# Block-sparse attention on attended blocks alone in F32 tiles, with an f16 first product in the feed-forward part

## The chip, the cores and the metric

One core of one Trainium2 chip. The metric is the device time of one launch in microseconds (us). The kernel before took 909.31 us (median of 3 runs, 909.0 to 910.31).

## The reference

`q`, `k`, `v` are 4 batches x 8 heads x 768 tokens x 64, in float32; `sampled_blocks` gives 3 random key blocks for each of 24 query blocks of 32 tokens.

```python
scores = scale * np.matmul(q, k.transpose(0, 1, 3, 2))
mask = np.abs(blk_i - blk_j) <= 1
mask = mask | (blk_i == 0) | (blk_j == 0) | (blk_i == n_blocks - 1) | (blk_j == n_blocks - 1)
for qb in range(n_blocks):
    for kb in sampled_blocks[qb]:
        mask[qb * 32:(qb + 1) * 32, kb * 32:(kb + 1) * 32] = True
scores = np.where(mask, scores, -1e9); scores -= scores.max(-1)
attn = np.exp(scores); attn /= attn.sum(-1) + 1e-9
x = (attn @ v) as 3072 tokens x 512
h = x @ w_in                      # 512 x 2048
out = (h - np.tanh(h)) @ w_out    # 2048 x 512
```

So the first and last query block see all 24 key blocks, and each of the other 22 sees at most 8: itself and its two neighbours, the two end blocks, three random ones.

## The kernel before, in words

There are two stretches in one program. In the first, attention runs head by head, and a part of the feed-forward work is woven in; in the second, only feed-forward work is left.

Attention before computes all 768 x 768 scores of a head, with the mask as extra rows of the product. Values are split in a high and a low half, so that two or three products at the faster matmul rates stand for one float32 product. For each head `smax` (L479) makes scores with the queries on the partitions, `maxima` (L485) takes their row maxima, `scores` (L520, L521) makes them again with the keys on the partitions and the maximum taken off in an extra row. Then ScalarE exponentiates 128 x 768 at a time (`expo`, L527) and makes an f16 high half (`p_high`, L531), GpSimd makes the low half (`p_low`, L540), and `accum` (L563, L566, L567) multiplies by V in f16, 36 products of 65 columns for a step. One step is 256 keys of one head; there are 96 steps. `norm` (L574 to L578) divides by the sums and `spill` sends the result to DRAM (`xscr`), from where the feed-forward part loads it.

The feed-forward part cuts the tokens in 6 chunks `n` of 512 and the 2048 hidden columns in 16 tiles `ft`. One unit is (n, ft). Its first product is 12 matmuls of 512 columns (`h_part`, L915, three split products for each of four rows of `w_in`, in fp32r), its gate is 5 instructions on VectorE, 5 on ScalarE and one on GpSimd (`g_part`), its second product is 12 matmuls (`o_mm`, L950 to L952). All of `w_in` and `w_out` come as 64-bit words; VectorE turns each tile to float32 in three instructions (`convert_part`), and the tile is then split. Before, 4 tiles are made in the first stretch (`NRES`), two more are stored, and 10 are made in the second (`RATE` gives how many per unit). 16 of the 96 first products are in the first stretch, and 14 of the second ones. Segments (`SEGS`) give the order of the 82 units of the second stretch.

The order on each engine is written out (`ORDER`, one string an engine), and the engines wait for each other by semaphores. Nothing of the second stretch is put ahead of anything of the first on any engine. DMAs are issued by SyncE, one after the other, in that order too. `KeepBusy` puts idle matmuls on ones (L245) where the planner expects TensorE to be idle.

Of the kernel before, what the change touches and what calls it, by code (L numbers as in the profile page):

```python
# [22 lines left out]
P = 128  # L23
B, H, S, D = 4, 8, 768, 64
NB, BLK = 24, 32
T = S // P
# [6 lines left out]
SEGS = ((3, 2, 6), (4, 0, 6), (5, 0, 16), (4, 6, 16), (3, 6, 16), (2, 4, 16), (1, 4, 16), (0, 4, 16))  # L33
RATE = 1.0
# [6 lines left out]
        "#$%#%#%#%######)()##+&##$$&#%##'&####)($$#%##*%)##(##))&#++#'&(#'##''##&)(##+*'#,##*'&###*')##(##%##%##$#+%###"  # L41
        "$#%*##(%#*#&###(###'#&#%##*%##$#+####'####((#################$$$%##$$$###$######$$$%%''&''&(#&%%#%%%%%#%%&&%#$"
        '%#$,$$$####&#$#&####2$$$$###$$#$#$$+#%%$#$$#%$$#$$###%%#######%%####%###################$$%%$#&$#%%$$$&#$$#$$%'
        "%$##########$###$$%%%%%%&&&#&&'&&##%%&&%#$#%##%##(%$###############$#$$#(##$$#*&$$%%$#$$$#$$###%#$##########*%"
        "%$$$##$$##$$#%%##$$##$$#%&&$#'###%%##$%%#*#&&$#$#$$#'########%#$###%#$#(%##&###$&$$#$#$###$#%##&%'##'##%%###%#"
        "#&#####$###$$$%##%%##%%$%%#######/#$$##)%#+&#(%#$&##%#%#%#(#&#($'##'$'$#&&###''$%+%$($&####$%%#$(#$%###('&$#$#"
        "$&%#$$'#&$####$%#&###$#%$#'&%(##&#%###%)&#%$#&#$%)'$%('#')$#&'#$#&%&###%#%##%$%&&'$%&'#%###$#%#&##%#&%##$$##%&"
        "$'#'$##&%##&&*$&#(##%'$##(##*$%##$#(#&%#'#$#$$#&$#&$#%$#'&%$##%%)%$###(#%()$###)'#%#)'$)&##&#%#($%#$''$#%(#&)#"
        "$#&$($'#$&''$#)$#$*$##+$$$#&)#(#%$%##&%%(($%###&&$#'#*%%'$#$'#$%)&##'#$$#%$(%$##(%%##(#+$#$#&*#($&#((###(##&%)"
        "'$###(#&*###&#)##&##%'#%#(#&$)$#'%##&##$&#$'##$&#%$##"  # L50
    ),
    "ACT": (
        "####$#$$$%$&&$###%$&$##(%$$#%%##$#%$$'###$$##%$$##$#+#'%%$##%%#$#&#%$##&$%#$%##%$#%##*##%$##%#$##'#%$#%$###'$%"
        "&#$&%#+##&%%###%$$'##$%$$#$$###$$/###%#$#$####%$%$(%%'&#&&#%'&%####%/&&$$&&&&(#&#&%'#%###%&$$#%##%$#$$#+#*#$#'"
        "##$(#$#%%#%##%$##%##4##$$#%$#$#&%#%$#$##$##$##%######-##$#$#$#$#%$'$(&$&#%&#%%%%#$##1&&#%#'##&%%#%%&%#%%&#$#&%"
        "$##$#$#%$###$*#%$&&###($#%%$##%$$##%$###%%%##($#%$##%#'$#%&%$###%$'&$$(%$&%$#$#$$#$#$#)#&%%$#'#'$##$$&$$$#$#%$"
        "#&1%#%$##&$#%%##$$&$####&$%##$#%%#'#$#%$#$$#%##$#%#$#$'$'$')&$%$&,%+$##,#$*##-%$#$#$$$$#,,$$%##($#&#%$#$#$###("
        "''))'##%#$###$##'#%#'$$%&%##('##%#($$'&&$#)($$&$%$&&&##$&&$%%#)$%%%#$($&&$%(''$$#$'&&$%(''%#%'''%)&#'#&$#'$&&$"
        "#$&&&$#$'&&$%(%&#%#$$&%)%$$#%#$$%$$$'$####%&#$#%#%&%###$$$##$$###%$###%$$##$%$$#%####$$'$$$###&#$$##%####%$###"
        "###'##$$##%$##&%#$$#%####$$##&#$#&##$$$#%###&#$####$##%&####%$###%$$$#$$###$%$$#$$##&%#$#%&#$##%$#&##$###%$$##"  # L60
        "$##'&#%#$$##$&##$$$#$$##%#$##&#$$$#$#$#%%###%%#$$#$%$##%##'##$$$#%$$#%####%%%#$#%####$$####$#'#%#####"
    ),
    "DVE": (
        "$########'#&#%####%#&####&#((#(%#%&%#('##$##$#((#'$'##$$&##$##$##)*##$#'#$'####$###$#(#''#'##$%$######$##$#$$%"
        "%(#'##%##$')'##%'##&#$##$#$$##$####'#$#'#&$#$#'&#%6###337#66-#)####%####$#+#**%#*%#$$&$#(#%%'#$$%%(&&($'$#%###"
        "'#(&#%#&#%####$########$#'%#($#&$%##'&##$#$##*#,&&####$#$##%%##$#$%%$$$######$###$%%#$$'#&#&#$$)$$#&####$#&#&$"
        "#$#&#####$$$##$##%%#%#####$$$''$#&$%#%%%$%%####%$$%$$%$#$$$$$#''''((#&#%#$#))#(--####)$##)#####$###&#'###$#*##"
        "####%#$#&&###$$###$##$$$$###%%%*#$##'#%%%*%%#''###$#'#&&&&#((#'#&##(##&&&&##'#&&#%#$#&&&#%%##&&&#%%#'#&&#%#(($"
        "#&&#%##&&&&#%##&&#%###'##%%%%#$####$#######&#############$####$############################%#####'$$#$###%####"
        "####&###########$##############$####$#####'%#%%$$%$$##################$##################%#$###########&###&&&"  # L70
        '$$############$$#################################$####$$##(##&&&&&%#$$$####################################%#$'
        '####$$##'
    ),
# [1140 lines left out]
```

## Time and profile before

| | |
|---|---|
| median of 3 runs | 909.31 us |
| span of the profiled execution | 907.1 us, 2.2 us less than that median |
| TensorE busy, granted clock | 888.4 us (98%), 1.00 |
| VectorE busy | 693.4 us (76%) |
| ScalarE busy | 650.2 us (72%) |
| GpSimd busy | 492.7 us (54%) |
| DMA | 120.74 MB, mean 133 GB/s |
| chain that ended last | TensorE 81%, VectorE 7%, ScalarE 4%, DMA 2% |

The span is the time from the first to the last instruction of the profiled execution. Busy time of matmuls counts each from its start to its modelled end, and successive matmuls overlap; what a matmul takes of TensorE is read from the distance between the starts of successive ones.

### The profile page before, as it was taken

To read this page: it belongs to the slowest core of one execution; us is meant where nothing else is said; L and a number is where in the kernel's file an instruction comes from. 1 tells how busy PE (TensorE), PEld (TensorE's weight loads), DVE (VectorE), ACT (ScalarE), POOL (GpSimd) and SP (SyncE) were. 2 spreads that over 40 slices of the span, in tenths; PEclk is the share of its full clock that TensorE was granted. 3 is DMA by queue.
4 is the path that set the end of the run, shared out by engine and by line. 5 is a ranking of instruction groups with operands and counts; after the bars stand their busy time and mean duration, and the time that the engine had idled before them with its cause. 6 is when DMAs were issued, how large, how long until landed. Compare 5 with 4: busy or idle time off the path is not lost.

```text
span 907.1 us, 18330 instructions
## 1 busy us (share of the span) xinstructions
PE 888.4 (98%) x7167; PEld 741.4 (82%) x7167; DVE 693.4 (76%) x998; ACT 650.2 (72%) x982; POOL 492.7 (54%) x328
## 2 busy tenths in 40 slices
PE   7999999999999999999999999999999999999998
PEld 4788888788888888888878878788888888888886
DVE  5799988899788877797479999876576666766664
ACT  5989998888888898798856766565555555555553
POOL 5899987778776887678923345432222222222221
PEclk9999999999999999999999999999999999999999
DMA  8897866877876667766333333230043103300301
GB/s 209 200 232 217 226 179 178 203 207 208 232 219 169 185 151 227 191 170 183 119 110 102 108 93 94 70 116 1 1 175 115 41 8 128 105 0 1 106 1 46
DMA packets 59406, 120.74 MB, mean 133 GB/s; under 512 B 6362, under 2 KB 27028, under 8 KB 58808
## 3 DMA queue, kind: packets, MB, share of 16 engines
q1 hardware_dynamic: 59320, 119.58, 46.4%
q8 instruction: 56, 0.92, 0.4%
q14 instruction: 30, 0.25, 0.1%
HBM read 55.68 MB, written 26.21 MB: 90 GB/s over the span
## 4 chain that ended last, share of the span: by engine, by line
PE 81%; DVE 7%; ACT 4%; DMA 2%; POOL 1%; issue 1%; SPq 1%; ACTq 0%; DVEq 0%; POOLq 0%
PE bank L915 26%; PE pf L950 8%; PE pf L952 7%; PE pf L951 7%; PE pst L520 6%; PE pst L521 5%; PE psm L479 5%; PE pav L563 3%; PE pav L566 3%; PE pav L567 3%; DVE mc L485 2%; ACT pe L527 2%; DMA slab<-hm 2%; PE bank L950 1%; PE bank L951 1%; PE bank L952 1%
## 5 line engine op out<-in xcount | busy, mean ns | idle before, releaser
L540 POOL TENSOR_TENSOR ph<-pe,ph 128x768 f16<-128x768 f32 x192 | 317.0, 1674 | 79.2 <-ACT ph L531 38.8
L945 POOL TENSOR_TENSOR gl<-t,gh 128x512 fp32r<-128x512 f32 x96 | 124.0, 1293 | 301.8 <-ACT gh L943 252.2
L485 DVE TENSOR_REDUCE mc<-psm 128x2 f32<-128x1536 f32 x93 | 162.9, 1752 | 26.2 <-PE psm L479 25.9
L527 ACT ACTIVATE pe<-pst 128x768 f32<-128x768 f32 x174 | 140.7, 809 | 40.5 <-PE pst L521 34.4
L531 ACT ACTIVATE ph<-pe 128x768 f16<-128x768 f32 x192 | 158.1, 841 | 3.8 <-PE pav L567 2.4
L520 PE MATMUL pst<-slab 128*128 128x512 f32 x348 | 126.2, 363 | 4.6 <-ACT pe L527 2.3
L929 DVE TENSOR_TENSOR t<-t,bank 128x512 f32<-128x512 f32 x96 | 65.6, 683 | 84.4 <-ACT t L927 55.4
L563 PE MATMUL pav<-vhl,ph 128*128 128x65 f16 x1152 | 115.8, 193 | 0.0
L566 PE MATMUL pav<-vhl,ph 128*128 128x64 f16 x1152 | 115.0, 195 | 0.0
L567 PE MATMUL pav<-vhl,ph 128*128 128x65 f16 x1152 | 114.6, 192 | 0.0
L935 ACT ACTIVATE u<-u,bias 128x512 f32<-128x512 f32 x96 | 69.3, 722 | 59.6 <-DVE bank L937 58.4
L521 PE MATMUL pst<-slab 97*128 97x512 f32 x348 | 110.9, 340 | 0.0
L563 PEld LDWEIGHTS <-ph 128*128 128x128 f16 x1152 | 105.3, 96 | 6.5 <-issue 3.6
L566 PEld LDWEIGHTS <-ph 128*128 128x128 f16 x1152 | 106.6, 97 | 0.1
L567 PEld LDWEIGHTS <-ph 128*128 128x128 f16 x1152 | 106.6, 99 | 0.0
L479 PE MATMUL psm<-slab 88*128 88x512 f32 (+1 forms) x378 | 88.3, 350 | 5.0 <-DMA slab<-hm 2.1
L927 ACT ACTIVATE t<-bank 128x512 f32<-128x512 f32 x96 | 56.8, 592 | 49.4 <-PE bank L915 33.7
L941 DVE COPY_PREDICATED t<-u,bank 128x512 f32<-128x512 int32 x96 | 71.5, 745 | 19.6 <-ACT u L935 14.5
L943 ACT ACTIVATE gh<-t 128x512 fp32r<-128x512 f32 x96 | 60.0, 627 | 34.8 <-DVE t L941 27.0
L520 PEld LDWEIGHTS pst<-slab 128*128 128x128 f32 x348 | 65.8, 189 | 21.7 <-ACT pe L527 7.4
L925 ACT ACTIVATE u<-bank 128x512 f32<-128x512 f32 x96 | 56.9, 593 | 36.8 <-PE bank L915 34.1
L939 DVE SCALAR_TENSOR_TENSOR bank<-qq,bank 128x512 f32<-128x512 f32 x96 | 66.5, 693 | 16.4 <-ACT qq L933 10.6
(154 smaller groups left out, 1988.8 us busy)
## 6 DMA issues: line engine op xcount, KB each, us to landing
slab<-hm SPq DMA_DIRECT2D x124, 192.0 KB
slab<-lo SPq DMA_DIRECT2D x63, 192.0 KB
raw<-qk SPq DMA_DIRECT2D x15, 768.0 KB
stage<-w_in SPq DMA_DIRECT2D x16, 512.0 KB
stage<-w_out SPq DMA_DIRECT2D x16, 512.0 KB
xsav<-xbuf SPq DMA_DIRECT2D x16, 512.0 KB
rawv<-v SPq DMA_DIRECT2D x16, 384.0 KB
xscr<-xq SPq DMA_DIRECT2D x16, 384.0 KB
```

The costliest lines, as they stand in the source:

```text
L479: nc.tensor.matmul(o[:, b0 + c0 : b0 + c1], lhsT=sB[s][0:88, t * P : (t + 1) * P], rhs=sA[s][0:88, c0:c1], start=True, stop=True)
L485: nc.vector.tensor_reduce(out=mcs[h][:, t - 1 : t + 1], in_=psm.rearrange("p (x s) -> p x s", x=2), op=ALU.max, axis=AX.X)
L520: nc.tensor.matmul(o, lhsT=sC[c][:, kc], rhs=sD[c][:, c0:c1], start=True, stop=False)
L521: nc.tensor.matmul(o, lhsT=sA[a][0:97, kc], rhs=sB[a][0:97, c0:c1], start=False, stop=True)
L527: nc.scalar.activation(out=o[:, c0:c1], in_=area[:, 0 : c1 - c0], func=AF.Exp, scale=0.125)
L531: nc.scalar.activation(out=halves(s)[:, x, 0], in_=pe[s % 2][:, c], func=AF.Copy)
L540: eng.tensor_tensor(out=pl, in0=pe[s % 2][:, c], in1=ph, op=ALU.subtract)
L563: nc.tensor.matmul(oav[:, t, :], lhsT=ph[:, c], rhs=vv[:, 0:65], start=(kt == 0 and t == 0), stop=False, skip_group_check=True)
L566: nc.tensor.matmul(oav[:, t, 0:64], lhsT=ph[:, c], rhs=vv[:, 65:129], start=False, stop=False, skip_group_check=True)
L567: nc.tensor.matmul(oav[:, t, :], lhsT=pl[:, c], rhs=vv[:, 0:65], start=False, stop=last, skip_group_check=True)
L915: self.nc.tensor.matmul(h, lhsT=w[:, cc], rhs=z[:, c, :], start=(c == 0 and x == 0), stop=(c == NCT - 1 and x == 2))
L945: nc.gpsimd.tensor_tensor(out=gl, in0=t, in1=gh.bitcast(F32), op=ALU.subtract)
```

## The change

Attention is made anew. Q, K and V stay float32 with no split. Query blocks are put in the order 0, 23, 1, 2, ... by the host, so that a tile of 128 queries (`m`) is either the two end blocks with blocks 1 and 2 (m = 0) or four inner blocks (m = 1 to 5). A step is one (m, pair of heads), of which m = 0 takes two; there are 112 steps, 28 a batch. For m > 0 each of four query blocks and two heads has its own 256 keys, and each product uses a 64 x 32 piece of the array. K of a batch is whole on chip (`kt`); GpSimd copies the end blocks and the three random blocks of a query block into `kg`, the latter at addresses in registers. V rows of neighbours and random blocks come by DMA into `vg`, the latter from addresses in registers (`v_rand`, on SyncE and ScalarE). The probabilities are turned by TensorE (`p_turn`), copied out of PSUM (`p_copy`) and multiplied by V in float32.

In the feed-forward part the first product's operands are f16 high and low halves with scales by powers of two, 6 weight tiles are made in the first stretch, 22 first products and 20 second ones are there, and 76 units are left for the second stretch. The scales add VectorE work to each `w_in` tile (`scale_ops`, `col_op`). The result of attention goes to the feed-forward part on chip for the first 4 chunks. The strings of `ORDER` are new. Cut to the core:

```diff
-SEGS = ((3, 2, 6), (4, 0, 6), (5, 0, 16), (4, 6, 16), (3, 6, 16), (2, 4, 16), (1, 4, 16), (0, 4, 16))
-RATE = 1.0
+SEGS = ((3, 2, 6), (4, 0, 6), (5, 0, 16), (4, 6, 16), (3, 6, 16), (2, 6, 16), (1, 6, 16), (0, 6, 16))
+RATE = 2.0
+NQ, NX, NK, NV, NE, NPH = 5, 5, 8, 6, 3, 3
+    def k_rand(b, i, j):
+        if j == ACTJ:
+            load_reg(i, j, "POOL")
+        nc.gpsimd.tensor_copy(
+            out=kg[:, kslot(b, i), 1 + j].rearrange("p y c -> p (y c)"),
+            in_=kt[b % 2].rearrange("p n y c -> p n (y c)")[:, bass.ds(regs[i, j, 1], 1)]...)
+    def v_rand(b, i, j):
+        src = v[b].rearrange("(n p) e -> n p e", p=BLK)[bass.ds(regs[i, j, 0], 1)]...
+        eng = nc.scalar if j == ACTJ else nc.sync
+        eng.dma_start(out=vg[BLK * j : BLK * j + BLK, vslot(b, i), 1], in_=src)
+    def scores(b, m, pr, s):            # m > 0
+            for c in range(4):
+                i, q0 = 4 * m - 1 + c, m * P + BLK * c
+                for near in range(2):
+                    for r, h in enumerate(half):
+                        n = slice(0, 96) if near == 0 else slice(96, 256)
+                        mm(o[32 * c : 32 * c + 32, r, n], lhsT=qq[h, q0 : q0 + BLK], rhs=keys(b, i, h, y, near),
+                            tile_position=(64 * r, 32 * c), **w)
+        # m == 0: two heads, 64 end queries, 512 + 256 keys, at (64 r, 64 r); then blocks 1 and 2
+        for n0, n1 in ((0, 16), (16, 24)):
+            for r, h in enumerate(half):
+                mm(flat[h, n0 * BLK : n1 * BLK], lhsT=qq[h, 0:64], rhs=kk, tile_position=(64 * r, 64 * r), **w)
...
+    def p_turn(s):
+        for i in range(4):
+            nc.tensor.transpose(pt[:, i * P : (i + 1) * P], pe[s % NE][:, i * P : (i + 1) * P], ident)
+    def accum(b, m, pr, s, z):          # m > 0: 2 heads x 2 halves x 4 blocks, 65 columns each
+                        one(slice(32 * c, 32 * c + 32), r, vg[:, g[c], zz], lhs, ...)  # tile_position=(0, 32 c)
-        self.xbuf = [cst.tile([P, 4096], F32R, name="xbuf0"), self.slab[:, 0:4096]]
+        self.xbuf = [cst.tile([P, 4096], F16, name="xbuf0"), None]
-                    w[x][ft] = tile(f"w{m}{x}{ft}", F32R)
+                self.wi[x][ft] = tile(f"wi{x}{ft}", F16)
```

## Rows read from the trace of the kernel before

**Rows 1.** Busy time by stretch: PE, PEld, DVE, ACT, POOL, then clock, DMA, GB/s.

```profile
0.00:50.00 50.00, 43.44 (x405) 31.66 (x405) 33.88 (x54) 36.96 (x54) 36.32 (x28) 1.00 0.84 209
...
13.00:455.00 442.00, 430.88 (x5158) 370.77 (x5159) 357.46 (x476) 385.85 (x541) 356.15 (x217) 1.00 0.73 196
455.00:610.00 155.00, 153.65 (x686) 124.69 (x685) 135.87 (x215) 98.96 (x169) 60.24 (x47) 1.00 0.32 99
```

**Rows 2.** Waits of PE up to 450 us, then after: total, times, longest.

```profile
PE pst L520 <- ACT pe L527: 2.3, 10, 0.3
...
PE pf L892 <- DMA wx<-xscr: 0.9, 1, 0.9
```

**Rows 3.** Timeline of PE, first and second stretch: start us, us, instructions in order.

```profile
10.86 0.38 PE L411 MATMUL bank<-ident,pe 128*97 128x128 f32 x2
...
13.53 0.59 PE L520 MATMUL pst<-slab 128*128 128x512 f32 x1
...
302.62 0.28 PE L521 MATMUL pst<-slab 97*128 97x256 f32 x1
302.74 0.20 PE L563 MATMUL pav<-vhl,ph 128*128 128x65 f16 x1
...
303.82 0.20 PE L567 MATMUL pav<-vhl,ph 128*128 128x65 f16 x1
303.86 0.27 PE L493 MATMUL psm<-ident,mc 128*6 128x128 f32 x1
303.88 0.48 PE L520 MATMUL pst<-slab 128*128 128x512 f32 x1
304.20 0.40 PE L521 MATMUL pst<-slab 97*128 97x512 f32 x1
...
307.45 0.60 PE L892 MATMUL bank<-ident,stage 128*128 128x128 f32 x4
307.81 0.95 PE L479 MATMUL psm<-slab 88*128 88x512 f32 x4
...
453.66 5.73 PE L915 MATMUL bank<-xbuf,hm 128*128 128x512 f32 x24
...
702.60 2.88 PE L915 MATMUL bank<-slab,hm 128*128 128x512 f32 x12
705.32 0.39 PE L950 MATMUL pf<-wx,gh 128*128 128x512 f32 x1
```

**Rows 4.** Groups by line: busy us, mean ns of one, idle time before.

```profile
L411 PE MATMUL bank<-ident,pe 128*97 128x128 f32 x12 | 2.5, 285 | 0.2 <-DVE pe L490 0.2
L485 DVE TENSOR_REDUCE mc<-psm 128x2 f32<-128x1536 f32 x93 | 162.9, 1752 | 26.2 <-PE psm L479 25.9
L435 DVE TENSOR_REDUCE sb<-psm 128x1 f32<-128x128 f32 x15 | 4.3, 289 | 7.6 <-PE psm L431 7.6
L577 DVE RECIPROCAL rs<-rs 128x6 f32<-128x6 f32 x32 | 6.1, 192 | 1.1
L578 DVE TENSOR_TENSOR xq<-pav,rs 128x384 f32<-128x384 f32 x32 | 17.8, 557 | 1.1
L945 POOL TENSOR_TENSOR gl<-t,gh 128x512 fp32r<-128x512 f32 x96 | 124.0, 1293 | 301.8 <-ACT gh L943 252.2 <-issue 43.1 <-PE bank L915 6.5
masks.py:199 POOL TENSOR_SCALAR_AFFINE_SELECT ident<-ident 128x128 f32<-128x128 f32 x1 | 0.3, 292 | 0.0
```

**Rows 5.** Timeline of VectorE back to back, then of SyncE's DMA issues.

```profile
533.44 0.69 DVE L931 TENSOR_TENSOR bank<-bank,u 128x512 f32<-128x512 f32 x1
534.04 0.69 DVE L813 SCALAR_TENSOR_TENSOR pf<-stage,pf 128x512 int32<-128x512 int32 x1
...
2.37 1.14 SPq L330 DMA_DIRECT2D raw<-qk  x2
```

**Rows 6.** Chain that ended last, at two places: start us, us, what.

```profile
459.83 2.47 DMA wx<-xscr
...
903.46 0.69 DVE spare L1011
```

More of the change, by code (lines that the diff above doesn't have):

```diff
@@ L45 @@
[L45 to L49, printed above, removed]
@@ L54 @@
[L54 to L58, printed above, removed]
@@ L186, in order, with moves @@
         bar = queue = 0.0
+        slots, moved = [0.0] * 8, 0
+        def moves(o):
+            return o[2] == "SP" and o[3] >= 0.05 or o[2] == "ACT" and o[4].__name__ in self.LOADS
         kind = 0
@@ L248, in before @@
                 )
+        if name == "accum":
+            b, m, pr, s, z = o[5]
+            self.used = True
+            self.since = 1e9 if pr % 2 and (m or z) or not (m or z) else 0.0
         self.free = max(self.free, t + o[3])
@@ L288, in attention_ffn @@
         keep = KeepBusy(nc, ones, pav)
-        k = 0
-        while k < len(ops) and not ops[k][9]:
-            if ops[k][2] == "PE":
-                keep.before(starts[k], ops[k])
-            ops[k][4](*ops[k][5])
-            k += 1
+        i = 0
+        while i < len(ops) and not ops[i][9]:
+            keep.before(starts[i], ops[i])
+            ops[i][4](*ops[i][5])
+            i += 1
     with ExitStack() as fctx:
         ffn.open(fctx)
-        for o in ops[k:]:
+        for o in ops[i:]:
@@ new lines, in attention @@
+    sc = [ps.tile([P, 2, 512], F32, name=f"sc{i}") for i in range(2)]
+    pt = ps.tile([P, 512], F32, name="pt")
+    av = ps.tile([P, 512], F32, name="av")
+    tile = lambda name, shape, dt=F32: acst.tile([P, *shape], dt, name=name)
+    kt = [tile(f"kt{i}", [NB, 4, BLK]) for i in range(2)]
+    qt = [tile(f"qt{i}", [S]) for i in range(NQ)]
+    kg = tile("kg", [NK, 5, 4, BLK])
+    vd = tile("vd", [T, HV])
+    vg = tile("vg", [NV, 2, HV])
+    pe = [tile(f"pe{i}", [512]) for i in range(NE)]
@@ new lines, in attention, with load, due_of @@
+    add = plan.add
+    def load(due, f, args, w, dur):
+        add(due, "SP", dur, f, args, w=w)
+    add(-42.9, "SP", 0.5, lambda: nc.sync.dma_start(out=xq[0][:, 0 : 6 * NB + NTAB], in_=blocks), w=[("xq", 0)])
+    add(-39, "DVE", 3.6, setup, r=[("xq", 0)], w=[("xq", 1), ("ix",)])
+    def due_of(b, m, y):
+        return 28 * b + (2 * y if m == 0 else 4 * (m + 1) + y)
+    first_use = lambda i: due_of(0, (i + 1) // 4, 0)
+    for i in range(1, NB - 1):
+        d = max(first_use(i) - 9 + 0.05 * i, -30 + i)
+        for z, eng, dur, hf in ((0, "SP", 0.02, 5), (0, "ACT", 0.45, False), (1, "POOL", 0.7, False)):
+            w = [("reg", z, i, j) for j in range(3) if (j == ACTJ) == (eng == "ACT")]
+            add(d, eng, dur, load_regs, (i, eng), [("ix",)], w, half=hf)
@@ L1048, in plan_early @@
+        for n, (b, gap) in enumerate(CHUNK):
+            sb = [("sb", i) for i in range(512 * n // S, (512 * n + 511) // S + 1)]
+            nk = NRES if n < 3 else 4
+            add(b - 1.96, "DVE", 0.3, self.x_scale, (n,), sb, [("sx", n)])
+            add(b + 1.9, "DVE", 0.3, self.cc_row, (n, 0, NRES), [("sx", n)] + [("sw", k) for k in range(NRES)], [("cc", n, k) for k in range(NRES)])
             for j in range(CT):
@@ L1076, in unit_ops @@
+                    add(s + 0.8 * room, "DVE" if g else "ACT", dve(512) if g else act(512), self.o_out, (n, g, j, bank[i]), [("bank", i)] + [("spare", j)] * (g > 0), [("spare", j)])
+                    if n < 3 and g == ng - 1:
+                        add(s + 0.81 * room, "SP", 1.05, self.put_part, (n, j), [("spare", j)], [("part", n, j)])
     def unit_ops(self, plan, f, n, ft, h, hq, xi, k, g, gi, halves, first=None, **kw):
@@ L1129, in plan_rest @@
+                add(d + 0.02, "DVE", dve(512), self.turn, (n, j, 2, i), xt + [("xh", i), ("sx", n)], [("xl", i)], **late)
+        conv = [(m, ft) for ft in range(NRES, NFT) for m in "io"]
         for x, (m, ft) in enumerate(conv):
@@ L1146, in plan_rest @@
                 m, i = SEGS[x + 1][0], 1 - xi
-                add(d, "SP", 6.1, self.get_x, (m, i), [("xsav", m, q) for q in range(4)], [("xh", i), ("xl", i)], **late)
+                add(d, "SP", 3.2, self.get_x, (m, i), [("xsav", m, q) for q in range(4)], [("xh", i), ("xl", i)], **late)
             g = ft % 4 if x == 0 else (u + 1) % 3
```

1067 lines of the change are left out of this document (468 added, 599 removed).

## The prediction

> **What bounds the kernel now.** First the busy time by stretch [rows 1]. TensorE is busy in 430.9 of 442 us of the attention stretch and in 153.7 of the next 155, at clock 1.00; VectorE has 357.5 and 135.9, ScalarE 385.9 and 99.0, GpSimd 356.2 and 60.2. Then the waits: the longest total that TensorE has before 450 us is 2.3 us, after it 0.9 us [rows 2]. So TensorE's instructions are the time, and the change is worth what it takes from them, unless something else becomes late.
>
> Where the stretches divide: the first 24 matmuls of the second start at 453.66, the chain's last instruction at 903.46 [rows 3, 6]. The second stretch is thus 449.8 us, the first 453.7, and 907.1 - 903.5 = 3.6 us are tail. The median is 2.2 us over the span; I add these.
>
> What a matmul takes is the distance of starts. Twelve fp32r products of 512 columns take 705.32 - 702.60 = 2.72 us, 0.2267 each; one of 256 takes 302.74 - 302.62 = 0.12, so a column costs (0.2267 - 0.12)/256 = 0.417 ns, which is 2.4 GHz, and an fp32r product 13 ns besides. The 36 f16 products of 65 columns take 303.86 - 302.74 = 1.12, 31 ns each, 4 ns over their columns. A float32 product leaves two records, and the pair of 128 columns takes 0.38 where one record is 0.285 long: the second starts 0.1 us behind, two cycles a column. So float32 costs 4 cycles a column. Four transposes take 307.81 - 307.45 = 0.36; a change of shape costs 304.20 - 303.88 - 0.23 = 0.09 [rows 3, 4].
>
> **The second stretch.** Before: 80 first products and 82 second ones, 1944 matmuls x 0.2267 = 440.7, and 8 x 0.36 = 2.9 of transposes, 443.6; 6.2 of its 449.8 us are stalls, most of them at its start. After: 76 units, of which two have their first product done. An f16 product of 512 columns is 512 x 0.417 + 4 = 217.5 ns (lower end 213.5, upper end the fp32r price). 74 x 12 x 0.2175 = 193.1, 76 x 12 x 0.2267 = 206.8, transposes 2.9, ten float32 products of 128 columns 2.1: 405. Six units fewer is most of it.
>
> VectorE is near its limit there: 135.9 of 155 us while ten tiles are made [rows 1], with successive starts 0.60 apart [rows 5]. The scales add for each `w_in` tile a reduction of 512 (0.6), one of 128 (0.29) and five small ones at 0.15 to 0.19 [rows 4], 1.7 us, 17 in all: 153 in a stretch that shrinks to 149 by fewer cycles of the first product. So 4 us of stall at least; I take 3 to 8 on top of the old 6, and 414 for the stretch (405 to 422).
>
> **The first stretch, TensorE.** For m > 0 a step has 16 score products, 8 of 96 and 8 of 160 columns, at places (64 r, 32 c) of the array. No row of before uses a part of the array. If the eight places work beside each other, a step takes (96 + 160) x 4 x 0.417 = 0.43 us; one after the other, 3.4. Its 16 V products of 65 columns at four places take 0.43 or 1.7, and transposes 0.36. I take the low ends, since the products read and write different partitions, and keep the others as rivals. 80 steps x 1.22 = 98. For m = 0, 16 pairs: scores 512 + 256 columns twice beside each other and four more places, 1.71; V products 16 in series of 0.108, 1.73; transposes 0.72; sum 4.16 x 16 = 67. Three to four changes of place or shape a step, 0.09 by the row, 0.16 if the array has to run empty (a product's 390 ns less its 227); I take 0.16: 112 x 3.5 x 0.16 = 63. Attention is 228.
>
> Feed-forward work there: 22 first products x 2.61 = 57.4; 20 second ones x 2.72 = 54.4; 16 x 0.36 and six small = 7: 119. TensorE needs 347 in all, where before it was busy 431.
>
> **The first stretch, what ends last.** VectorE: row maxima 80 x 0.8 and 16 x 1.4; two of three `p_copy`, 74 x 0.6; 48 `norm` x 0.75 (192 and 557 ns rows, 256 elements for 384); gates 22 x 3.1; twelve weight tiles x 2.4 with scales 8; input halves and outputs 40 x 0.6; maxima of V 13, setup 4: about 320. ScalarE comes to 230 by the same way, GpSimd to 211: 264 copies at 0.29 (the row of 128 elements) and 0.35 for the register that I guess between an issue gap of 0.05 and a DMA issue of 0.57, 32 copies of ends and 22 low halves x 1.29 [rows 4]. SyncE issues some 375 DMAs at 0.57 [rows 5], 214. None reaches 347, so TensorE's work is the floor, and order and latency add to it:
>
> Start: 2 MB of K and Q and 1.6 MB of V must be there before the first V product, at the 209 GB/s of the opening [rows 1] 17 us; before, the first scores for good began at 13.53 [rows 3]. I take 16 us in which little is done.
>
> The first 20 steps have no chunk ready and make the weights: VectorE has 1.5 us of attention and 1.85 of weights a step: 20 x 3.35 = 67.
>
> 52 steps carry the feed-forward units: 119 + 52 x 2.04 = 225, TensorE bound.
>
> 40 steps are attention alone. There V must be refilled: of the three pairs of slots a group of four steps uses two, so one pair waits for the group before. After the last V product of a group SyncE issues five DMAs (2.9) and the last lands 2.5 after [rows 6]; four V products and a `norm` take 3: 8.4 a group, 2.1 a step, 84 us (82 by TensorE alone; 104 if the refill slips by 2 us).
>
> Sum: 16 + 67 + 225 + 84 = 392 (lower end 16 + 347 = 363; upper end 430, with 0.6 us more a step in the steps without feed-forward work). Total: 392 + 414 + 3.6 + 2.2 = 812; ends 363 + 405 + 5.8 = 774 and 430 + 414 + 5.8 = 850.
>
> **The rivals.**
> Small products limited by their number. Scores and V products leave 64 records a step. The nearest row is 31 ns from pair to pair of weight load and product [rows 3]: 1.98 us instead of 0.86, 80 x 1.12 = 90 more (for m = 0 the columns are longer than that). TensorE then needs 437, the idle share goes, stretch 463, total 883. For: float32 makes two records of each; against: the 31 ns row is 27 ns of columns, so its own limit isn't shown. The Trainium skill (TensorE: Matmul & The Clock Gate, Wait — 56ns, not 53.3ns?) gives about 25 ns as the least distance of starts; by that, an estimate, it would be 59 us more, and no row here shows a shorter distance.
>
> Row pieces in one bank. For m = 0 the two heads write to the same bank from upper and lower rows of the array; if they take turns, 16 x 1.71 = 27 us more, total 839. Nothing in the rows speaks for or against, since all products there use all rows. The Trainium skill (TensorEngine Tiling (Array Packing), Restrictions and Gotchas) says that different row tiles cannot access one PSUM bank at the same time; no run here shows it yet. For m > 0 the heads have a bank each, and that rule changes nothing.
>
> Feeding. GpSimd's register loads could cost more. The first stretch may last 907.1 - 414 - 3.6 = 489 before the gain is gone; less 16 us of start and 42 of other work, 264 copies may cost 1.63 each, 1.34 of it for the register. At 0.9 each GpSimd is the bound: 264 x 1.19 + 42 + 16 = 372, still hidden; at 1.2 it is 452, total 872.
>
> No concurrency: slower. If pieces of the array work one after the other, m > 0 takes 5.1 instead of 0.86, 80 x 4.28 = 342, and m = 0 3 us more a pair, 48: the first stretch becomes 16 + 347 + 390 = 753, total 1173. It decides against the change from 126 of these 390 us on (489 - 16 - 347). Against it: nothing in the trace; for it: no product there shows two at once. It also stands for the change not doing what it says, since skipping two thirds of the scores pays only if pieces run together.
>
> **How the numbers follow.** Forecast (774 to 850) 0.60; one bank (839, inside that range) 0.10; limited by number (883) 0.15; feeding (850 to 1000) 0.05; no concurrency 0.05; below 774, if weights and V hide behind more than I see, 0.05. The range 776 to 888 holds the first three but for their edges, 0.83. Faster by over 0.2% (1.8 us, about what a measurement tells): 0.60 + 0.10 + 0.15 + 0.05 and half of feeding, 0.92; slower: no concurrency and the rest of feeding, 0.07; between, 0.01.
>
> **What would show it.** The second stretch at 405 to 422 us with TensorE over 96% busy, first products 2.56 to 2.61 apart by twelve; if VectorE shows under 97% there, the scales cost nothing. In the first stretch, starts of scores of a step within 0.5 us (right), 1 us (number) or 3.4 (no concurrency); for m = 0, 1.7 or 3.4. TensorE's waits should be led by VectorE in the first 20 steps and by the V DMAs in the steps of attention alone; a wait led by GpSimd's copies would be the feeding rival. I am wrong if the clock falls in the gaps, since all prices are from rows at 1.00.

## The result, and the profile after

The changed kernel takes 871.48 us (median of 4 runs, 865.89 to 874.71), the kernel before on the same chip 909.15; the ratio is 0.959, 95% interval 0.955 to 0.964. That is 4.1% less where 10.7% was forecast (812 us); the time lies above the 774 to 850 that the forecast's sum gave, and inside its wider range of 776 to 888. The profiled run took 868.49 us, its span is 866.6.

The split first. These are TensorE's timeline at the end of the first stretch and VectorE's last instruction of the second (start us, us, instruction, repetitions, the wait ahead of it in brackets).

```profile
428.93 1.15 PE L510 MATMUL av<-vg,ph 128*32 128x65 f32 x64 [0.25 <-DVE xq L541]
430.02 1.25 PE L814 MATMUL bank<-xbuf,wi 128*128 128x512 f16 x5
...
862.51 0.69 DVE L904 SCALAR_TENSOR_TENSOR spare<-pf,spare 128x512 f32<-128x512 f32 x1 [0.81 <-PE pf L852]
```

| | before | forecast | after |
|---|---|---|---|
| first stretch | 453.7 | 392 | 430.0 |
| second stretch | 449.8 | 414 | 432.5 |
| tail and rest of the run's time | 5.8 | 5.8 | 6.0 |

So of the 57 us that are missing in this run, 38 lie in the first stretch and 18.5 in the second. Busy time by stretch of the kernel after (PE, PEld, DVE, ACT, POOL, clock, DMA share, GB/s; compare [rows 1]):

```profile
0.00:50.00 50.00, 42.01 (x524) 23.96 (x532) 40.52 (x98) 15.75 (x30) 12.36 (x47) 0.93 0.82 253
50.00:100.00 50.00, 29.86 (x869) 21.00 (x857) 43.20 (x96) 17.48 (x38) 9.90 (x38) 0.89 0.75 216
100.00:430.00 330.00, 311.02 (x5889) 214.53 (x5871) 248.46 (x521) 170.74 (x335) 83.72 (x239) 1.00 0.56 158
...
450.00:550.00 100.00, 89.49 (x393) 55.61 (x393) 95.78 (x179) 63.03 (x103) 37.27 (x30) 0.98 0.29 93
...
600.00:860.00 260.00, 258.28 (x1143) 161.59 (x1143) 175.94 (x257) 150.65 (x237) 61.19 (x48) 1.00 0.16 52
```

Three regimes: up to 100 us VectorE and the DMA engines are busy and TensorE is half idle from 50 us on, at a lower clock; then TensorE works 311 of 330 us; from 450 to 550 VectorE is busy 96% and TensorE 89%. Only after 600 us is the second stretch TensorE's alone. PE's waits up to 100 us, from 100 to 430, and after that (total, times, longest; compare [rows 2]):

```profile
PE pt L385 <- DVE ph L503: 9.3, 1, 9.3
PE bank L740 <- DVE wam L736: 4.8, 2, 4.4
...
PE pt L497 <- ACT pe L493: 3.1, 3, 1.9
PE av L510 <- issue: 3.0, 3, 1.3
PE pt L497 <- DVE ph L503: 2.8, 4, 1.0
...
PE bank L814 <- DVE t L841: 5.9, 9, 2.3
PE pf L740 <- DVE wam L736: 3.1, 2, 1.9
PE pf L850 <- DVE spare L904: 2.6, 2, 2.4
```

None of TensorE's waits names GpSimd's copies. These copies of random blocks take 297 ns each and GpSimd is busy 26% of the span, so the feeding rival falls by the trace alone. The costs that the forecast sized, in the groups by line (busy us, mean ns of one, idle before):

```profile
L417 POOL COPY kg<-kt 128x128 f32 x264 | 69.3, 297 | 169.5 <-PE sc L453 109.2 <-PE sc L467 28.4 <-issue 25.8
L766 DVE SCALAR_TENSOR_TENSOR cc<-sx,sc,sign 128x6 f32<-128x6 f32 x20 | 9.5, 520 | 0.0
L736 DVE TENSOR_REDUCE wam<-ob 128x1 f32<-128x512 f32 x10 | 6.8, 678 | 0.0
L668 DVE TENSOR_REDUCE sc<-pf 128x1 f32<-128x128 f32 x10 | 2.8, 284 | 0.5 <-PE pf L740 0.5
```

Last, TensorE's timeline: two steps of scores of m > 0 (their first record, one in the middle, the next instruction after them), one pair of m = 0, and the second and first products of the second stretch.

```profile
255.39 0.43 PE L453 MATMUL sc<-kt,qt 64*32 64x96 f32 x15
...
256.33 0.50 PE L453 MATMUL sc<-kg,qt 64*32 64x160 f32 x9
256.76 0.66 PE L791 MATMUL bank<-ident,xq 128*128 128x128 f32 x4
...
131.29 1.51 PE L461 MATMUL sc<-kt,qt 64*64 64x512 f32 x8
132.72 0.39 PE L467 MATMUL sc<-kt,qt 64*32 64x96 f32 x8
132.91 0.47 PE L467 MATMUL sc<-kg,qt 64*32 64x160 f32 x8
133.32 0.50 PE L850 MATMUL bank<-wo,gh 128*128 128x512 f32 x1
...
704.22 0.39 PE L852 MATMUL pf<-wx,gl 128*128 128x512 f32 x1
704.45 0.40 PE L850 MATMUL pf<-wx,gh 128*128 128x512 f32 x1
704.69 0.39 PE L851 MATMUL pf<-wx,gh 128*128 128x512 f32 x1
704.92 0.40 PE L852 MATMUL pf<-wx,gl 128*128 128x512 f32 x1
705.16 2.76 PE L814 MATMUL bank<-xbuf,wy 128*128 128x512 f16 x12
707.57 0.58 PE L850 MATMUL pf<-wx,gh 128*128 128x512 f32 x1
```

Two steps take 256.76 - 255.39 = 1.37 us, 0.69 each; one behind the other it would be 3.4 each, so pieces of the array do work beside each other. For m = 0 the long products take 132.72 - 131.29 = 1.43 us, where columns alone are 1.28 and two heads in turn would be 2.56: sharing a bank costs next to nothing. The second products are (705.16 - 704.22)/4 = 0.235 apart (233 ns on the mean of some 740), where [rows 3] have 0.2267. The first ones take 2.41 for twelve starts up to the early start of the next, and 216 ns each, as forecast (217.5).

### The profile page after: what moved, and what is told of

It is laid out like the page before. It is cut to its first block, busy times and chain, and to the rows that moved or that the text cites. A ratio compares the mean times of both kernels' runs of the same rounds, so it can differ in the third digit from the quotient of the medians.

```text
span 866.6 us, 23686 instructions
## 1 busy us (share of the span) xinstructions
PE 800.5 (92%) x9095; PEld 519.0 (60%) x9095; DVE 665.3 (77%) x1252; ACT 462.8 (53%) x813; POOL 225.8 (26%) x418
## 4 chain that ended last, share of the span: by engine, by line
PE 57%; DVE 24%; issue 7%; ACT 4%; DMA 4%; POOL 1%; SPq 1%; ACTq 1%; POOLq 0%; DVEq 0%
PE bank L814 17%; PE av L510 7%; PE pf L850 5%; PE pf L851 5%; PE pf L852 5%; PE sc L453 5%; PE pt L497 4%; DVE t L829 3%; DVE bank L831 3%; PE bank L850 2%; DVE bank L837 2%; DVE bank L839 2%; DVE mx L475 2%; DVE t L841 2%; PE bank L852 2%
## 5 line engine op out<-in xcount | busy, mean ns | idle before, releaser
L814 PE MATMUL bank<-xbuf,wy 128*128 128x512 f16 x720 | 165.2, 380 | 5.5 <-DVE t L841 5.4
L493 ACT ACTIVATE pe<-sc,mx 128x256 f32<-128x256 f32 (+1 forms) x208 | 89.8, 490 | 85.6 <-DVE mx L481 52.4
L829 DVE SCALAR_TENSOR_TENSOR t<-bank,cc,t 128x512 f32<-128x512 f32 x96 | 71.8, 748 | 75.8 <-ACT u L825 38.7
L417 POOL COPY kg<-kt 128x128 f32 x264 | 69.3, 297 | 169.5 <-PE sc L453 109.2
L850 PE MATMUL pf<-wx,gh 128*128 128x512 f32 x240 | 105.0, 437 | 0.6 <-DVE ob L906 0.4
L814 PE MATMUL bank<-xbuf,wi 128*128 128x512 f16 x432 | 100.1, 380 | 1.6 <-DVE t L841 1.2
L851 PE MATMUL pf<-wx,gh 128*128 128x512 f32 x240 | 94.9, 395 | 0.0
L852 PE MATMUL pf<-wx,gl 128*128 128x512 f32 x240 | 94.7, 394 | 0.0
L475 DVE TENSOR_REDUCE mx<-sc 128x2 f32<-128x512 f32 (+1 forms) x112 | 75.3, 684 | 22.6 <-PE sc L453 13.9
L497 PE MATMUL pt<-ident,pe 128*128 128x128 f32 x448 | 71.5, 282 | 11.3 <-DVE ph L503 4.2
L831 DVE SCALAR_TENSOR_TENSOR bank<-bank,cc,u 128x512 f32<-128x512 f32 x96 | 72.1, 751 | 4.6 <-ACT u L825 4.4
```

Of the source, the lines that this page charges most:

```text
L475: red = lambda i, j: nc.vector.tensor_reduce(out=i, in_=j, op=ALU.max, axis=AX.X)
L493: nc.scalar.activation(out=dst, in_=i, func=AF.Exp, scale=SCALE, bias=o[:, 1, r : r + 1])
L497: nc.tensor.transpose(pt[:, i * P : (i + 1) * P], pe[s % NE][:, i * P : (i + 1) * P], ident)
L814: self.nc.tensor.matmul(h, lhsT=w[:, cc], rhs=z[:, c, :], start=(c == 0 and x == 0), stop=(c == NCT - 1 and x == 2))
L829: nc.vector.scalar_tensor_tensor(out=t, in0=h, scalar=minus, in1=t, op0=ALU.mult, op1=ALU.add)
L831: nc.vector.scalar_tensor_tensor(out=h, in0=h, scalar=c, in1=u, op0=ALU.mult, op1=ALU.mult)
```

## The experiments

Each kernel is the changed one with the edit shown. The first stretch is taken up to the first product after the last V product, and the second from there to the start of the last product (432.1 us in the changed kernel). A kernel is judged by stretch and not by its total alone, and the first stretch is cut once more by a marker: the start of the 600th of the 3200 records of V products, when some 22 of 112 steps are through. Each stretch is read from one profiled execution, and they spread. In the seven kernels whose edit leaves the work of the first stretch as it was it took 430.0 to 440.6 us: the marker came at 102.7 to 108.4 us, and from there to the end it took 327 to 335. The second stretch took 431.8 to 432.9 in the eight kernels without an edit there. A difference that lies within these spreads shows nothing.

**VectorE's scales in the second stretch** (the early return stands in `w_max`, `w_all`, `w_scale` and `cc_col`; `cc_row` then makes the columns of all 16 tiles at once).

```diff
     def w_max(self, ft, src):
+        if ft >= NRES:
+            return
...
+        tc.nc.vector.memset(self.swr[:, NRES:], 2.0**16)
+        tc.nc.vector.memset(self.rsw[:, NRES:], 2.0**-16)
```

> The ten w_in tiles that are made in the second stretch get a fixed scale of 2 to the 16th: their reduction of 512 columns, the product that spreads it, the reduction of 128, the three small steps and the two small products of scales are left out (a scale fixed in advance stands in for one computed from the weights; it is the one part left out). VectorE theory: it was 97% busy from 450 to 550 us and loses 10 x 2.6 to 3 us there, so TensorE's 14.3 us of waits in the second stretch fall to 4 or less and the stretch from 433 to about 421; total about 860. Rival, TensorE is limited by its own products and the order, and the waits only move: stretch 430 or more, total 868 or more.

Measured: 859.96 us, ratio 0.946 (0.943 to 0.949), 11.5 us under the changed kernel. The second stretch took 419.0, TensorE's waits there 7.5 us in place of 14.8 (4 or less was expected). The same 100 us as above, of this kernel:

```profile
450.00:550.00 100.00, 94.68 (x425) 58.30 (x424) 92.03 (x145) 69.64 (x114) 39.88 (x32) 1.00 0.32 101
```

TensorE has 425 records for 393, and its clock stays at 1.00. The VectorE theory holds for the stretch: the scales are worth 13 us of it. Of these, 7.3 are TensorE's waits. The other 5.8 are its own work, the stretch less the waits (432.1 - 14.8 = 417.3 and 419.0 - 7.5 = 411.5): the ten products that spread the maxima go, 2.3 us by the distances of starts, and the products that are left take 3.4 us less, at a clock of 1.00 in place of 0.98 from 450 to 550 us. The scales cost VectorE more than was forecast (its timeline in the changed kernel):

```profile
489.48 1.45 DVE L766 SCALAR_TENSOR_TENSOR cc<-sx,sc,sign 128x6 f32<-128x6 f32 x2
490.84 0.68 DVE L662 SCALAR_TENSOR_TENSOR ob<-stage,pf 128x512 int32<-128x512 int32 x1
```

The two small products take 1.36 us up to the next instruction; with 0.6 for the large maximum, 0.32 for the small one and 3 x 0.19 that makes 2.85 us a tile where I had 1.7.

**Second products: where operands begin.** The first kernel has the pad ahead of the weight tiles, the second the other first products in `h_part`, the third both:

```diff
+        pad = cst.tile([P, 16], F32, name="pad")
...
+        if half is None and n < 3:
+            for c in range(12):
+                cc = slice(c % 4 * P, c % 4 * P + P)
+                matmul(h, lhsT=wo[0][0][:, cc], rhs=wo[1][0], start=c == 0, stop=c == 11)
+            return
```

> One small tile of 64 bytes per partition is put ahead of the resident weight tiles, so that every w_out half begins at an odd multiple of 64 bytes, as in the kernel before; now they begin at multiples of 128. Nothing else changes. Addresses theory: the second products come from 233 ns apart (trace of the changed kernel) to 226.6 (kernel before), 912 x 6.5 ns = 5.9 us less in the second stretch, 433 to about 427, and the total from 871.5 to about 865. Mixing theory (f16 and fp32r products in turn): the distance stays at 233 ns and the total at 871.5 but for run to run spread.

> The first products of the last three groups of units (chunks 2, 1 and 0, 30 units, some 160 us) are replaced by twelve fp32r products of 128x512 of two w_out halves; the result of those units is thus not the reference's, and everything else runs as in the changed kernel. No f16 product stands between the second products there. Mixing theory: from where that part begins, all products come 226.7 ns apart as in the kernel before, and before it they stay at 233. Addresses theory: the second products stay at 233 ns all through. If the second products fall to 226.7, a unit takes 5.44 us in place of 2.59 + 2.80 = 5.39, so the total moves by +1.5 us at most.

> Both edits on the second products together: the 64 bytes ahead of the weight tiles, and fp32r first products in the last three groups of units (their result is not the reference's). So far: 233 ns with neither, 229.4 with the shift, 230.8 with one type. If addresses and mixing are two causes that add, 226.7 in the last three groups as in the kernel before, where both held. If they are one cause in two forms, or a third thing is needed, 229 or more.

Means of distances: 229.4 ns with the shift (873.49 us, ratio 0.960, 0.954 to 0.965), 230.8 with one type and 226.9 with both (one execution each, 878.88 and 882.31 us, with first stretches of 436.4 and 440.6). That looked like two causes that add, and the rows say otherwise. With one type and no shift:

```profile
741.99 0.40 PE L855 MATMUL pf<-wx,gh 128*128 128x512 f32 x1
742.23 0.39 PE L856 MATMUL pf<-wx,gh 128*128 128x512 f32 x1
742.46 0.40 PE L857 MATMUL pf<-wx,gl 128*128 128x512 f32 x1
742.70 2.89 PE L814 MATMUL bank<-wo,wo 128*128 128x512 f32 x12
745.43 0.40 PE L855 MATMUL pf<-wx,gh 128*128 128x512 f32 x1
745.66 0.39 PE L856 MATMUL pf<-wx,gh 128*128 128x512 f32 x1
```

The second products are still (742.70 - 741.99)/3 = 0.237 apart, and only the products that stand in for the first ones go at (745.43 - 742.70)/12 = 0.2275: 230.8 is a mean of two kinds. With the shift alone:

```profile
738.71 0.40 PE L853 MATMUL pf<-wx,gh 128*128 128x512 f32 x1
...
740.56 0.39 PE L852 MATMUL pf<-wx,gh 128*128 128x512 f32 x1
...
743.05 0.39 PE L854 MATMUL pf<-wx,gl 128*128 128x512 f32 x1
743.28 1.04 PE L816 MATMUL bank<-xbuf,wy 128*128 128x512 f16 x4
```

The first ones after f16 products are 0.231 apart (738.71 to 740.56, eight), the later ones 0.2267 (740.56 to 743.28, twelve). So the shift settles them, and a change of type costs only the first few. The operands' first addresses, worked out from the order of the tiles in the program (the trace does not show them), say why it could be so: in the slow case the gate tiles begin at an odd multiple of 64 bytes and the w_out halves at a multiple of 128; in the fast cases both are odd (before, shift) or both even (the stand-ins, two w_out halves). One more kernel moves the gate tiles, and the second pad keeps the weights at multiples of 128:

```diff
+        pads = [cst.tile([P, 16], F32, name="pad0")]
         self.g = [[tile(f"g{x}{i}", F32R) for x in "hl"] for i in range(4)]
...
+        pads.append(cst.tile([P, 16], F32, name="pad1"))
```

> Nothing is left out. 64 bytes stand ahead of the gate tiles (the stationary operands of the second products) and 64 more behind them, so that gate tiles and w_out halves both begin at multiples of 128; in the changed kernel the gate tiles begin at odd multiples of 64 and the w_out halves at multiples of 128, with the 64 bytes ahead of the weights alone both begin at odd multiples. Difference theory: the second products are slow when the two operands differ in this; they settle at 226.7 ns, 229 to 230 on the mean since the first five after a change of type are slower, as with both odd. Place theory: the w_out halves alone must begin at odd multiples; 233 ns as in the changed kernel.

```profile
745.85 0.39 PE L855 MATMUL pf<-wx,gh 128*128 128x512 f32 x1
...
747.93 0.39 PE L855 MATMUL pf<-wx,gh 128*128 128x512 f32 x1
...
750.19 0.39 PE L856 MATMUL pf<-wx,gl 128*128 128x512 f32 x1
```

229.1 ns on the mean, 0.231 for the first nine (745.85 to 747.93) and 0.226 for the next ten (747.93 to 750.19); 871.05 us, ratio 0.956, 0.951 to 0.961. The difference theory held, the place theory fell. The other mix, gate tiles at a multiple of 128 and w_out halves 64 bytes off, was not run. In time it is little. The second stretch is 431.8 and 430.3 with the two shifts, where the products gave back 3.5 us: 431.8 is no difference, and TensorE's waits there grew from 14.8 to 15.9 and 15.8. The mixing theory of the first two expectations is wrong in the form I gave it, and the addresses theory was right in the cause and off by half in the size.

**The first 100 us.**

```diff
+        for e, name, before in (("DVE", "v_max", 79), ("DVE", "v_scale", 91), ("PE", "v_all", 60)):
+            j = lanes[e].index(v1[name])
+            lanes[e].insert(before - 1, lanes[e].pop(j))
```

> Only the place of three instructions changes: the maximum of batch 1's V on VectorE stands 18 instructions later, its product on TensorE 17 places later, its scale 22 later, so that the DMA of that V (landed at 61.72 us) is there before VectorE comes to it. Queue theory: VectorE's wait of 3.37 us and TensorE's wait of 9.3 us at 58 to 68 us go; VectorE sets the pace there, so the first stretch gets shorter by 3 to 5 us (430 to 425 to 427) and the total is 866 to 868. Rival, the rest of the first 100 us is limited by another thing (DMAs, which are over 0.8 busy up to 75 us): another wait of 3 us or more takes its place, first stretch 429 or more, total unchanged.

In the changed kernel VectorE sits in front of a DMA with its whole queue behind it, and TensorE's 9.3 us follow from that:

```profile
58.20 0.15 DVE L677 TENSOR_SCALAR sc<-sc 128x1 int32<-128x1 int32 x1
61.72 3.35 DVE L382 TENSOR_REDUCE vm<-vd 128x1 f32<-128x3072 f32 x1 [3.37 <-DMA vd<-v]
```

With the maximum later, that wait is gone and two others are there that the changed kernel does not have, 7.2 us for TensorE's scores and 4.3 before the weights (VectorE's waits, 40 to 112 us, of that kernel):

```profile
DVE mx L482 <- PE sc L460: 7.2, 1, 7.2
DVE bank L661 <- DMA stage<-w_out: 4.3, 1, 4.3
```

877.02 us, ratio 0.965 (0.962 to 0.969): no gain, if anything a loss, and the first feed-forward product started at 116.5 (107.1 in the changed kernel). The rival held; the queue theory fell. So the traffic itself was cut, with all waits left in place:

```diff
 def load_w(nc, raw, w_in, w_out, m, ft):
+    if 0 < ft < NRES:
...
+        return nc.sync.dma_start(out=raw[:, 0:128], in_=w_out[ft * P : (ft + 1) * P, 0:128])
```

> The loads of the weights for resident tiles 1 to 5 (ten DMAs of 512 KB in the first 100 us) move an eighth of their columns or less; the instructions, their places and their waits stay, so SyncE's queue is as it was, and those weight tiles hold stale words (left out: 4.6 MB of weights). Traffic theory: DMA engines are over 0.8 busy up to 75 us at 230 to 275 GB/s, 4.6 MB are some 18 us of their time, and V rows, V for the maximum and weights all come late for that; the first feed-forward product starts 8 to 15 us earlier than its 107 to 112 us, the first stretch falls from 430 to 440 to about 422 to 428, and TensorE's wait of 6 to 10 us at V's maximum goes. Rival, VectorE's and SyncE's order: first product at 107 or later, first stretch 430 to 440.

```profile
25.00:75.00 50.00, 39.65 (x902) 28.11 (x906) 47.21 (x107) 19.55 (x41) 11.09 (x43) 0.90 0.66 182
```

The DMA share from 25 to 75 us fell from 0.82 to 0.66, and VectorE was busy 47.2 of those 50 us (45.2 before the cut). The marker came at 98.8 us (103.4 in the changed kernel, 102.7 to 108.4 in the seven named above), the first feed-forward product at 102.6, the first stretch ended at 425.4; total 867.61, ratio 0.957 (0.954 to 0.961). So traffic costs some 4 to 5 us there by this one execution, about half of what the theory said or less; with it gone VectorE is the bound, and TensorE's wait at V's maximum stays (6.0 us). The totals alone do not tell this kernel from the changed one.

**What sets the pace after that.** Scores with fewer records, and with fewer columns:

```diff
+                n0 = min(i - 1, NB - 8)
+                for r, h in enumerate(half):
+                    mm(
+                        o[32 * c : 32 * c + 32, r, 0:256], lhsT=qq[h, q0 : q0 + BLK], rhs=kt[b % 2][h, n0 : n0 + 8, y],
...
-                        n = slice(0, 96) if near == 0 else slice(96, 256)
+                        n = slice(0, 32) if near == 0 else slice(96, 128)
```

> For m > 0 each 32 queries of a head take one product of 256 columns of keys (eight neighbouring blocks) where they had one of 96 and one of 160: as many columns and half as many products, 32 records a step for 64 counting both of a float32 product's (the random and end blocks are left out of the scores, so the result is not the reference's; GpSimd's copies still run). Number theory: the price of a step's scores, 0.685 us in the changed kernel's trace, is 32 records x 21 ns; half the records fall to the bound by columns, 0.43, and 80 x 0.25 = 20 us leave a stretch in which TensorE sets the pace from 100 us on, so the first stretch falls by 12 to 20 us. Column theory: 0.685 stays and so does the time. Third, waits: TensorE gets shorter but the waits for ScalarE and VectorE (19 us from 100 us on) grow by as much, and the stretch falls by under 5 us.

> For m > 0 the two products of scores per 32 queries and head keep their number and take 32 columns each in place of 96 and 160 (three quarters of the scores are left out, so the result is not the reference's). Number theory: a step's scores still take about 0.67 us (32 records x 21 ns), and the first stretch moves by under 4 us. Column theory: a step falls to 0.11 to 0.2, 80 x 0.5 = 40 us of TensorE go, and the first stretch falls by 20 us or more.

Two steps of each kernel, from the first record to the next instruction; first half the records, then few columns:

```profile
251.26 1.09 PE L452 MATMUL sc<-kt,qt 64*32 64x256 f32 x32
252.29 0.33 PE L797 MATMUL bank<-ident,xq 128*128 128x128 f32 x1
```

```profile
253.66 0.29 PE L453 MATMUL sc<-kt,qt 64*32 64x32 f32 x10
...
254.23 0.24 PE L453 MATMUL sc<-kg,qt 64*32 64x32 f32 x4
254.40 0.44 PE L791 MATMUL bank<-ident,xq 128*128 128x128 f32 x2
```

1.03 and 0.74 us where the changed kernel takes 1.37. One step alone takes 0.64 in the changed kernel, so the step behind it adds 0.73; with half the records it adds 0.43 (1.025 - 0.592), the bound by columns; with a quarter of the columns 0.42 (0.747 - 0.325). Neither theory is right alone: columns and records both cost, the records some 0.3 us a step at full rate. Half the records gave 856.85 us, ratio 0.944 (0.940 to 0.948), and the first stretch ended at 420.2, 9.8 us earlier: more than the theory of waits said (under 5) and less than the number theory (12 to 20). Few columns took more from TensorE and gave nothing: 869.36, ratio 0.957, stretch 431.0. From 200 to 400 us TensorE was then busy 182.6 us at a clock of 0.98 where the changed kernel has 190.6 at 1.00; the rest went into waits. Three more kernels: no refill of V (the return stands in `v_ends`, `v_near` and `v_rand`) by itself, the same with few columns, and a shorter maximum with few columns:

```diff
     def v_rand(b, i, j):
+        if b:
+            return
...
-            red(o[:, 0], x[:, :, 0:256])
+            red(o[:, 0], x[:, :, 0:64])
```

> After batch 0 no V rows are fetched any more: the DMAs of v_near, v_ends and v_rand are left out for batches 1 to 3 and the slots keep batch 0's rows (so the result is not the reference's); some 240 of 320 issues and 22 MB go. V theory, the prediction's: the steps of attention alone wait for the refill, 2.1 us each or more, and without it fall to what TensorE needs, 1.8 to 1.9; from the 600th V record on (103 to 108 us) the first stretch takes 326 to 330 us in the runs so far and would take 310 to 318, the total falls by 10 to 16 us. Rival: TensorE's own work (311 us of it from 100 us on) and many short waits for ScalarE and VectorE set the pace, each under 2 us, and V is hidden: 322 us or more from the 600th record on, total 866 or more.

> The kernel of few columns (two score products of 32 columns each; three quarters of the scores of m > 0 left out) and besides no V fetched after batch 0 (both make the result another than the reference's). The few columns alone took 24 us from TensorE and gave the first stretch nothing: from the 600th V record on 328 us, as with all columns (326). V theory: the refill of V was what came late next, so with both gone that part falls to 312 or less and the total to 855 or less. Chain theory: scores, maximum, exponential, turn, copy and V product of a step follow each other through three engines in one written order, and that sets a pace of its own near 320: 318 or more, total 860 or more.

> The kernel of few columns with a shorter maximum besides: VectorE reduces 64 columns of a head in place of 256, so that some 0.4 us per step of m > 0 go (32 us of VectorE in all; the result is not the reference's). Chain theory, VectorE's part of it: the step's way from scores to exponential gets 0.4 us shorter and VectorE has room, so from the 600th V record on the time falls from 328 to 318 or less, and the first 100 us, where VectorE is over 0.8 busy, get 3 us or more shorter as well; total 858 or less. Rival (V's refill, the clock, or ScalarE): 323 or more from the 600th record on, total 865 or more.

| kernel | total | ratio to before | 600th V record | end of first stretch | between |
|---|---|---|---|---|---|
| changed | 871.48 | 0.955 to 0.964 | 103.4 | 430.0 | 326.6 |
| maximum later | 877.02 | 0.962 to 0.969 | 111.6 | 437.7 | 326.1 |
| small loads | 867.61 | 0.954 to 0.961 | 98.8 | 425.4 | 326.6 |
| half the records | 856.85 | 0.940 to 0.948 | 101.1 | 420.2 | 319.1 |
| few columns | 869.36 | 0.953 to 0.961 | 103.0 | 431.0 | 328.0 |
| no V refill | 866.21 | 0.949 to 0.956 | 107.2 | 429.9 | 322.7 |
| few columns, no V refill | 860.41 | 0.945 to 0.952 | 102.5 | 419.1 | 316.6 |
| few columns, short maximum | 865.54 | 0.950 to 0.956 | 99.7 | 420.7 | 321.0 |

In the kernels with this part untouched the last column is 326 to 335, so differences under some 8 us are not clear of the spread. V's refill alone is worth some 4 us of it or a little more: V is nearly hidden, as the rival said. With few columns, taking V away gives 11 us and the shorter maximum 7, neither all that its theory said (16 and 10), where few columns alone gave nothing. The shorter maximum also brought the marker from 103.0 to 99.7, the 3 us that its theory said. Half the records gave 7.5 us in the last column, all that its products gave up (18 joined pairs of steps x 0.35 and some 25 lone steps x 0.05: 7.5); few columns gave up some 19 by the same count (0.63 and 0.31) and the stretch kept none.

The waits and the clock from the marker on say where it went. In the changed kernel TensorE waits 19.0 us of the 326.6, at a mean clock of 1.00. With few columns its waits grow to 32.7 (6.3 of the 13.7 more are time in which the profile shows nothing that it waited for), and its own work falls by 12.5 and not by 19, at 0.984. Without V as well the waits are 28.0, with the shorter maximum 28.1, both at 0.995. So V and the maximum take under 5 us of the waits each; the rest of their gain, 6.5 and 2.2 us, is TensorE's own work at the higher clock. Some 28 us of waits stay with either gone: the nearer of the theories is that of the chain, a step's way through three engines in one written order (318 us or more and 860 or more, for the measured 316.6 and 860.4), but no run took that order apart. Why the clock differs, these runs leave open. Half the records also frees the scores from GpSimd's blocks; that this played a part was not tried.

**A better version.** Nothing left out: the later steps of the late scales (with the inverse) on GpSimd, and the 64 bytes ahead of the weights.

```diff
+        eng = self.nc.gpsimd if ft >= NRES else self.nc.vector
...
+    (eng or nc.vector).tensor_scalar(
+        out=si, in0=si, scalar1=float(bits << 23), scalar2=float(235 << 23), op0=ALU.add, op1=ALU.min
...
+            self.nc.gpsimd.tensor_scalar(
+                out=self.cc[:, x, :, ft], in0=self.rsx[:, 0:6], scalar1=self.rsw[:, ft : ft + 1], scalar2=1.0 - 2 * x,
```

> Nothing is left out. Two edits: for the ten late w_in tiles the second step of the power of two, its inverse and the two products of scales run on GpSimd (busy 17.6 of 50 us there) in place of VectorE, and 64 bytes stand ahead of the resident weight tiles. VectorE theory: it loses 0.19 + 0.19 + 1.2 = 1.6 us a tile, 16 in all, of the 26 to 30 whose removal gave 12 us; I expect 6 to 9 us for these, and 1 to 3 us for the second products at 229.4 ns in place of 233: second stretch 421 to 426 for 432, total 859 to 865. Rival, the port that GpSimd and VectorE share or the longer chain to the scale takes the gain back: second stretch 430 or more.

```profile
450.00:550.00 100.00, 92.26 (x404) 57.70 (x402) 91.47 (x157) 64.83 (x107) 43.20 (x58) 0.97 0.32 98
```

865.00 us, ratio 0.950 (0.946 to 0.954), the fastest of the kernels that leave nothing out; the second stretch took 426.0, at the slow end of the forecast, and VectorE is down to 91.5% there. The shared-port rival (430 or more) fell: the small products take 277 ns each on GpSimd, where VectorE took 520. The two edits were not run apart here; the shift alone moved this stretch by 0.3 us.

## Why the prediction was right or wrong

The sign was right, and so was the mechanism that carried it: row and column pieces of the array work beside each other, so the no-concurrency rival (1173) is out. The Trainium skill (TensorEngine Tiling (Array Packing), Restrictions and Gotchas) rules out one bank for two row pieces at the same time; this trace does not agree, 1.43 us for what in turn would be 2.56. The two heads write different partitions of the bank here, and no run had them on the same ones. The size was off, by these steps:

1. **"TensorE's work is the floor, and order and latency add to it", with nothing for latency in the steps that carry feed-forward work.** This is the step that failed in the first stretch. From the marker on, the forecast was 392 - 86.7 = 305 us (86.7 = 16 + 67 + 1.75 x 2.1, for the 21.75 steps through by then), nearly all TensorE's; it took 326.6, of which TensorE's work is 307.7 and its waits 19.0, none over 1.9 us. Work was close: a step of m > 0 costs 0.69 + 0.54 + 0.63 = 1.86 with its changes of shape (forecast 1.22 + 0.56 = 1.78), a pair of m = 0 5.0 (5.28), the feed-forward part about 9 us over its 119, much of it second products at 233 ns and more changes of type than I counted. The waits were the term left out, and no experiment found one cause that stands for them: they are 19.0 us with V's refill and 17.3 without. The 40 steps of attention alone, where the forecast had put its only wait, are no stage of the changed kernel: feed-forward products stand in every 20 us of the trace from 107 us on, and after the marker TensorE waits 0.1 us for a V DMA.

2. **The first 20 steps, 16 + 67.** The marker came 17 us late (103.4 for 86.7). VectorE as the bound was right (43 of 50 us), but its work was sized too low, 83.7 us busy in the first 100 with setup and two maxima of V, and I counted the opening's traffic for the first loads only. The small loads show that traffic at over 0.8 of the engines costs some 4 to 5 us of this. The clock did fall in the gaps, as the prediction named for its own undoing, but where VectorE set the pace; its share was not measured apart. The changed kernel's four runs took 865.9 and 868.5 us at a mean clock of 0.984 and 0.986, and 874.5 and 874.7 at 0.977 and 0.975; that is a link and not yet a cause.

3. **The scales, 1.7 us a tile, 17 in all.** They cost 2.85, and without them 13 us of the second stretch go. The mechanism was right, a term was mis-sized, and it explains the smaller part of the 18 us that are missing there: TensorE waits 14.8 us in that stretch, where the forecast of 414 had 9 and its upper end 14. The term: two small strided products with an operand from a column of scalars, 520 ns each, were priced like a row of 0.15 to 0.19.

4. **405 us of TensorE's own work in the second stretch, with 912 fp32r products at 226.7 ns.** This work took 417.3, the larger part of the 18. The fp32r products came at 233 in place of 226.7 ns, 5.9 us, from the beginnings of the operands; no row of before could show it, since all its operands of that kind begin alike. The clock of 0.98 from 450 to 550 us is some 2 more (an estimate, 0.02 x 100). Most of the rest stood in the trace before already: the prediction took 6.2 us of that second stretch for stalls, but TensorE's waits there are 1.2, so some 5 us were work that its prices left out. The f16 products were priced right (216 for 217.5 ns).

Of the rivals with one price, that of numbers was the nearest in time (883; its own sum, 16 + 437 + 414 + 5.8, gives 873) and half right: records cost, though not 31 ns each. 64 records in 1.37 us are 21 ns apart, and 64 short ones in 0.74 are 12. The Trainium skill (TensorE: Matmul & The Clock Gate, Wait — 56ns, not 53.3ns?) has about 25 ns as the least distance; with pieces of the array side by side the trace goes under it. The prediction's "no row here shows a shorter distance" was a misreading: [rows 3] have two starts 0.02 us apart (303.86 and 303.88). The feeding rival is out: no wait of TensorE names GpSimd's copies.

## What to carry to other kernels

When a change takes a tenth from the engine that is the bound, size the second and third in line stage by stage, down to the small strided instructions, and keep a term for waits that the old idle share does not show: after the change they meet. Read the first 100 us as a stage of its own, with the traffic of all that is loaded in it. And look at where the operands of the products begin before their price is copied from another layout.

## What the runs showed of the hardware

- fp32r products of 512 columns come 233 ns apart when the moving operand begins at a multiple of 128 bytes and the stationary one 64 bytes off, and settle at 226.7 when both begin alike, in either way; after f16 products the first eight or so take about 231 even then.
- Sixteen float32 score products on eight pieces of the array: 0.64 us alone, 0.73 behind another step; eight of them with the same columns 0.43 behind another.
- TensorE's granted clock was 1.00 through all of the trace before; after the change it is 0.89 from 50 to 100 us, where TensorE is busy 30 of 50, and 0.98 from 450 to 550. With few columns it was 0.98 from 200 to 400 us, busy 183 of 200.
- A product of 128 x 6 with an operand from a column of scalars, written 64 bytes apart, took 520 ns on VectorE and 277 on GpSimd; written in a row it took 276 on VectorE.
